# Chunked attention and a top-1 mixture of experts: row transposes placed between the halves of two matmul groups, and weight loads given to later groups

## The chip, the cores and the metric

The kernel runs on one core of a Trainium2 chip. The metric is the device time of one launch in microseconds (us); smaller is better. The engines named below are PE (matrix multiplies and transposes; PEld is its loading of weights), DVE (vector), ACT (scalar, activation), POOL (general purpose, it also issues the scattering and gathering DMAs) and SP (it only issues DMAs).

## The reference

Attention is computed in chunks of 64 positions, for 8 batches, 8 heads, 576 positions and a head size of 64. Its 4608 rows of 512 numbers go through a mixture of 8 experts, where each row uses only the expert with the largest gate logit.

```python
scores = scale * np.matmul(q_c, k_c.transpose(0, 1, 2, 4, 3))
attn = np.exp(scores - np.max(scores, axis=-1, keepdims=True))
attn = attn / (np.sum(attn, axis=-1, keepdims=True) + 1e-09)
x = np.matmul(attn, v_c)                    # -> rows: (4608, 512)
logits = x @ w_gate                         # (4608, 8)
expert_idx = np.argmax(logits, axis=1)
for e in range(8):
    xe = x[expert_idx == e]
    out[expert_idx == e] = gate_w * (np.maximum(xe @ w1[e], 0.0) @ w2[e])
```

Everything is float32. The experts' first layer is 512 to 1024 wide, the second 1024 to 512.

## The kernel before, in words

The rows are cut into 36 tiles of 128 and taken in 18 groups `g` of two tiles. One pass of the loop `for g in range(NG)` (line 1069) is a software pipeline in which four groups are under way. The names of its stages, with their lines:

- `scores(g)` (L255): 64 small matmuls of q and k into the two PSUM banks `psS`. The softmax follows on DVE and ACT: `soft_a` takes the maxima `mx` (L268) and subtracts them (`ex`, L271), `soft_b` is the exponential on ACT (L277), `soft_c` the sums `su` (L281), `soft_d` their reciprocals `ri` (L292).
- `attn_t` (L300) transposes the exponentials of group g-1 on PE, one PSUM bank for each tile, and ACT copies each bank to `at`.
- `attn_v` (L309) multiplies them by v into the banks `psU` and `psV`; `x_out` on DVE (L321, one instruction for each bank) scales them by `ri` and writes the rows `xb`.
- `x_t` (L332) transposes the rows of group g-2, one bank for each tile, and ACT copies them to `xT`; `logits` (L344) multiplies by the gate weights, and ACT copies the result `lp` (L1041).
- `sel_` (L1032) of group g-3 turns the logits into the layout of the routing, whose small steps (`advance`, `small_op`) lie on DVE; `store` (L451, POOL) scatters the rows to their experts' places `xd`, and after the 18 stores of the first batches gathers read them again (L583, POOL).

The transposes of `attn_t` use the banks U and V in the loop, those of `x_t` the banks T and Q. Every group reads 512 KB each of q (L208), k (L211) and v (L229) through SP's queue.

Beside this, the loop brings in the first expert's weights. `load_c(j)` (L1054) is one 512 KB DMA into half of a `raw` tile. The loads 0 to 3 are the first layer. `split_half` cuts each into two halves and each half into a rounded part `whi` (ACT, L88) and the rest `wlo` (POOL, L90), eight halves in all; the POOL part stands a group behind the ACT part. The loads 4 to 7 are the second layer and take the place of the raw first layer, so each has to wait until the `wlo` of its half is done. `loads` and `splits` say in which group each is called. From 124 us on PE also computes the first blocks of experts (L662) between the last groups, and from 161 us it computes nothing else.

On PE, DVE, ACT and POOL the instructions stand in the order of the code. On SP a scheduler decides the order: a load stands there as early as its waits let it, and not where the code calls it.

Of the kernel before, what the change touches and what calls it, by code (L numbers as in the profile page):

```python
# [8 lines left out]
F32 = mybir.dt.float32  # L9
# [9 lines left out]
P = 128  # L19
# [5 lines left out]
G = 2  # L25
NG = NTILE // G
RB = 4
XB = 5
# [21 lines left out]
def attn_moe_kernel(ctx: ExitStack, tc: tile.TileContext, q, k, v, wg, w, out):  # L50
# [192 lines left out]
            nc.tensor.matmul(pR.rearrange("p (a b) -> p a b", b=P), ones,  # L243
                             ones.unsqueeze(1).broadcast_to([P, 4, P]), start=True, stop=True)

    def scores(g):
        ps = pair
        if g == 3:
            nc.tensor.addr_align(64, offset=48, max_nops=0)
        for i in range(G):  # L250
            if g == 0 and i:
                keep(3)
            for hp in range(4):
                for po, m, fo, pi, fi, at_ in quads(i, hp):
                    nc.tensor.matmul(ps[po, m, fo], qt[g][pi, i, fi], kb[g % NK][pi, i, fi],  # L255
                                     start=True, stop=True, tile_position=at_)
        return ps
# [34 lines left out]
        nc.vector.reciprocal(ri.rearrange("p h o -> p (h o)"), suf)  # L292
        return ri

    def attn_t(ex, banks="UV"):
        at = sp.tile([P, G, 4, 128], F32, name="at", bufs=1)
        for i in range(G):
            pt = bank(banks, [P, 4, 128])
            for hp in range(4):
                nc.tensor.transpose(pt[:, hp, :], ex[:, i * 4 + hp, :, :].rearrange("p m k -> p (m k)"), ident)  # L300
            nc.scalar.copy(at[:, i, :, :], pt)
        return at

    def attn_v(g, at):
        px = [one["U"], one["V"]]
        for i in range(G):
            for hp in range(4):
                for po, m, fo, pi, fi, at_ in quads(i, hp):
                    nc.tensor.matmul(px[m][po, fo], at[pi, i, hp, po], vb[g % NB][pi, i, fi],  # L309
                                     start=True, stop=True, tile_position=at_)  # L310
        return px
# [12 lines left out]
                ri[:, m * NH // 2:(m + 1) * NH // 2, :].rearrange("p (i h) o -> p i h o", i=G)  # L324
                .broadcast_to([P, G, 4, 64]), ALU.mult)

    def x_t(g, xt):
        xT = sp.tile([P, 4, G * P], F32, name="xT1", bufs=1)
        for i in range(G):
            pxt = bank("TQ", [P, 4, 128])  # L330
            for kc in range(4):
                nc.tensor.transpose(pxt[:, kc, :], xt[:, (g * G + i) % RB, kc * 128:(kc + 1) * 128],  # L332
                                    ident)
            nc.scalar.copy(xT[:, :, i * P:(i + 1) * P], pxt)
        return xT
# [124 lines left out]
    def advance(kind, side=False):  # L460


        for x in active:
            if x[1] == kind and x[2] == side and not (kind == "t" and r_live[0]):
                x[1] = next(x[0], "end")
                if x[1] == "end":
                    active.remove(x)
                return
# [582 lines left out]
    def load_c(j):  # L1051

        c, s = j // 2, slice(j % 2 * F, (j % 2 + 1) * F)
        nc.sync.dma_start(raw[c % 2][:, s], w[c * E * P:c * E * P + P, s])  # L1054

    loads = {0: [1], 2: [2], 4: [3], 15: [4], 16: [5], 17: [6, 7]}
    splits = {g: [g - 1] for g in range(1, 9)}

    def cast(g):

# [3 lines left out]
        for j in loads.get(g, ()):  # L1064
            load_c(j)

    load_c(0)

    for g in range(NG):
        ga, gl = g - 1, g - 2  # L1070
        pace[0] = 1000
        if waiting:
            nc.gpsimd.tensor_copy(relay, st_l[gl - 1][:, 0:1])
        store(1 if g + 2 < NG else 4)
        ps = scores(g)
        keep((8, 6, 0)[min(g, 2)])

        if gl >= 1:
            sel_(gl - 1)
            advance("c")  # L1080
        if ga >= 0:
            at = attn_t(st_e[ga])
            if g + 3 < NG:
                hold_q(g + 3)
            su = soft_c(st_e.pop(ga))
        if gl >= 0:
            st_x[gl] = x_t(gl, xb[gl * G // RB % XB])
        if ga >= 0:
            soft_e(su)
        st_e[g] = soft_a(ps)  # L1090
        if g + 1 < NG:
            soft_b(st_e[g])
        else:

            c2.close()
            psum = ctx.enter_context(tc.tile_pool(name="psum", bufs=1, space=PSUM))
            slots["S"] = [psum.tile([P, 512], F32, name=f"psS{i}") for i in range(2)]
            turns["S"] = 0
        pauses()
        for x in casts:  # L1100
            next(x, None)
        casts.clear()
        advance("t")
        if g + 1 < NG:
            small_op(5)
        if ga >= 0:
            px = attn_v(ga, at)
        logits(gl)
        cast(g)
        if g + 1 == NG:  # L1110
            soft_b(st_e[g])
        if ga >= 0:
            ri = soft_d(su)
            x_out(ga, px, ri, xb[ga * G // RB % XB])
        small_op(2)
        advance("a")
        side_op(4)
        if waiting and g + 2 < NG:
            nc.gpsimd.tensor_copy(relay, st_e[g][:, 0, 0, 0:1])
            store(1)  # L1120
        if g + 3 < NG:
            load_q(g + 3)
        if 3 <= g + 2 < NG:
            load_v(g + 2)
        if g + 3 < NG:
            if gl >= 0:
                hold(kb[(g + 3) % NK])
            load_k(g + 3)
# [4 lines left out]
    make_xt(0, banks="SS")  # L1133
    small_op(5)
    ex = st_e.pop(g)
    at = attn_t(ex, "TQ")
    filler(1)
    su = soft_c(ex)
    soft_e(su)
# [220 lines left out]
```

## Time and profile before

| | |
|---|---|
| median of the runs | 579.99 us |
| profiled execution, its time | 575.24 us |
| its span (first to last instruction) | 573.1 us, granted PE clock 0.994 of full speed |
| PE, PEld busy | 95%, 83% of the span |
| DVE, ACT, POOL busy | 73%, 49%, 41% |
| chain that ended last, by engine | PE 83%, issue 7%, DVE 5%, DMA 2% |

The profiled execution lies 4.75 us under the median. "Issue" in a chain of waits is time in which an engine waited for nothing that the profile shows. A window is a stretch of the span, given by its first and last microsecond. In a row of a timeline, the brackets hold the idle time before the instruction and what ended it.

### The profile page before, as it was taken

To read this page: it belongs to the slowest core of one execution; us is meant where nothing else is said; L and a number is where in the kernel's file an instruction comes from. 1 tells how busy PE (TensorE), PEld (TensorE's weight loads), DVE (VectorE), ACT (ScalarE), POOL (GpSimd) and SP (SyncE) were. 2 spreads that over 40 slices of the span, in tenths; PEclk is the share of its full clock that TensorE was granted. 3 is DMA by queue.
4 is the path that set the end of the run, shared out by engine and by line. 5 is a ranking of instruction groups with operands and counts; after the bars stand their busy time and mean duration, and the time that the engine had idled before them with its cause. 6 is when DMAs were issued, how large, how long until landed. Compare 5 with 4: busy or idle time off the path is not lost.

```text
span 573.1 us, 14350 instructions
## 1 busy us (share of the span) xinstructions
PE 544.2 (95%) x5315; PEld 475.3 (83%) x5315; DVE 421.1 (73%) x886; ACT 278.2 (49%) x502; POOL 232.2 (41%) x272
## 2 busy tenths in 40 slices
PE   7698688899999999999999999999999999999995
PEld 4586667687689889898898999898999989899984
DVE  6789797995688887798877885667656566756654
ACT  1486555564163654456545553445425344544432
POOL 3114533366455445263542643152424226151422
PEclk9999998999999999999999999999999999999998
DMA  8989997843358452335625632466622346211201
GB/s 309 399 311 335 340 357 253 332 154 153 123 178 302 156 195 64 83 115 175 202 72 203 219 114 88 145 225 210 219 65 84 120 130 224 74 45 24 73 2 57
DMA packets 44852, 99.28 MB, mean 173 GB/s; under 512 B 12736, under 2 KB 26048, under 8 KB 41152
## 3 DMA queue, kind: packets, MB, share of 16 engines
q0 software_dynamic: 18352, 58.30, 29.3%
q1 hardware_dynamic: 26384, 39.36, 20.5%
q8 instruction: 83, 1.36, 1.0%
q14 instruction: 33, 0.27, 0.1%
HBM read 106.59 MB, written 20.22 MB: 221 GB/s over the span
## 4 chain that ended last, share of the span: by engine, by line
PE 83%; issue 7%; DVE 5%; DMA 2%; ACT 1%; POOL 1%; SPq 0%; POOLq 0%; DVEq 0%; ACTq 0%
PE psS L662 27%; PE psL L662 8%; PE psV L746 4%; PE psU L746 4%; PE psU L748 4%; PE psU L747 4%; PE psV L747 4%; PE psV L748 4%; PE psS L255 2%; PE psU L309 2%; PE psK L760 2%; PE psK L762 2%; DMA qt<-in_q 1%; PE psK L747 1%; PE psK L748 1%
## 5 line engine op out<-in xcount | busy, mean ns | idle before, releaser
L80 DVE TENSOR_TENSOR wlo<-raw,whi 128x1024 fp32r<-128x1024 f32 x114 | 138.8, 1218 | 14.6 <-ACT whi L79 14.1
L557 POOL DMA_INDIRECT raw<-in_w,widx x58 | 68.3, 1177 | 126.1 <-DVE wlo L80 57.8
L79 ACT CAST whi<-raw 128x1024 fp32r<-128x1024 f32 x114 | 118.8, 1043 | 0.0
L695 ACT ACTIVATE h<-psS 128x384 fp32r<-128x384 f32 x84 | 41.3, 492 | 158.8 <-issue 120.3
L662 PE MATMUL psS<-xhi,whi 128*128 128x256 f32 (+3 forms) x368 | 114.8, 314 | 0.1
L662 PE MATMUL psS<-xhi,wlo 128*128 128x256 f32 (+3 forms) x368 | 112.2, 307 | 0.0
L662 PE MATMUL psS<-xlo,whi 128*128 128x256 f32 (+3 forms) x368 | 106.3, 307 | 0.2 <-DVE xlo L613 0.2
L779 POOL DMA_INDIRECT out_y<-y,oid x40 | 43.0, 1076 | 100.3 <-ACTq L1247 34.6
L666 DVE SCALAR_TENSOR_TENSOR hl<-psS,h 128x256 fp32r<-128x256 f32 x84 | 35.5, 422 | 57.9 <-ACT h L695 57.8
L662 PEld LDWEIGHTS psS<-xhi,whi 128*128 128x128 f32 x368 | 69.4, 189 | 5.7 <-issue 1.6
L662 PEld LDWEIGHTS psS<-xhi,wlo 128*128 128x128 f32 x368 | 69.5, 189 | 4.0 <-issue 1.2
L575 POOL DMA_INDIRECT xg<-xd,idx x47 | 59.8, 1273 | 23.8 <-issue 12.2
L662 PEld LDWEIGHTS psS<-xlo,whi 128*128 128x128 f32 x368 | 67.6, 189 | 0.5 <-DVE xlo L613 0.4
L746 PE MATMUL psU<-whi,h 128*128 128x512 f32 x112 | 45.1, 403 | 0.0
L746 PE MATMUL psV<-whi,h 128*128 128x512 f32 x112 | 44.3, 396 | 0.0
L748 PE MATMUL psU<-whi,hl 128*128 128x512 f32 x112 | 44.0, 392 | 0.0
L747 PE MATMUL psU<-wlo,h 128*128 128x512 f32 x112 | 43.9, 392 | 0.0
L747 PE MATMUL psV<-wlo,h 128*128 128x512 f32 x112 | 43.8, 391 | 0.0
L748 PE MATMUL psV<-whi,hl 128*128 128x512 f32 x112 | 43.8, 391 | 0.0
L451 POOL DMA_INDIRECT xd<-xb,di x32 | 31.5, 986 | 14.0 <-issue 4.3
L662 PE MATMUL psL<-xhi,whi 128*128 128x384 f32 (+3 forms) x112 | 34.7, 310 | 0.2 <-issue 0.2
L255 PEld LDWEIGHTS psS<-kb,qt 64*64 64x64 f32 x1152 | 20.0, 137 | 17.8 <-issue 10.6
(259 smaller groups left out, 1133.8 us busy)
## 6 DMA issues: line engine op xcount, KB each, us to landing
vb<-in_v SPq DMA_DIRECT2D x18, 512.0 KB
kb<-in_k SPq DMA_DIRECT2D x17, 512.0 KB
qt<-in_q SPq DMA_DIRECT2D x17, 512.0 KB
xg<-xg SPq DMA_DIRECT2D x208, 32.0 KB
raw<-in_w SPq DMA_DIRECT2D x8, 512.0 KB
raw<-in_w,widx POOLq DMA_INDIRECT x58, 3.2
xg<-xd,idx POOLq DMA_INDIRECT x49, 3.9
out_y<-y,oid POOLq DMA_INDIRECT x40, 3.1
```

What stands on the lines that cost most here:

```text
L79: nc.scalar.copy(hi, src)
L80: nc.vector.tensor_tensor(lo, src, hi.bitcast(F32), ALU.subtract)
L451: landed[t] = nc.gpsimd.indirect_dma_start(out=xds[t], out_offset=bass.IndirectOffsetOnAxis(ap=di[:, i, :], axis=0), in_=x, in_offset=None ...
L557: nc.gpsimd.indirect_dma_start(out=raw[c][:, :], out_offset=None, in_=w, in_offset=bass.IndirectOffsetOnAxis(ap=widx[:, u, c:c + 1], axis= ...
L575: nc.gpsimd.indirect_dma_start(out=t[:, :], out_offset=None, in_=xd[0:rows, :], in_offset=bass.IndirectOffsetOnAxis(ap=place(u, h), axis=0 ...
L662: nc.tensor.matmul(ph, a[par][kc][:, f * 128:(f + 1) * 128], b[:, kc, at_:at_ + ph.shape[1]], start=kc == 0 and n == 0, stop=kc == 3 and n ...
L666: nc.vector.scalar_tensor_tensor(o, ph, 0.0, hi.bitcast(F32), ALU.max, ALU.subtract)
L695: nc.scalar.activation(hx[:, EXT:EXT + WIDE], ph, AF.Relu)
L746: nc.tensor.matmul(py, hh, wh, start=f == 0, stop=False)
L747: nc.tensor.matmul(py, hh, wl, start=False, stop=False)
L748: nc.tensor.matmul(py, hl, wh, start=False, stop=f == 7)
L779: nc.gpsimd.indirect_dma_start(out=outs[m], out_offset=bass.IndirectOffsetOnAxis(ap=oid[u % 3][:, m:m + 1], axis=0), in_=y, in_offset=None ...
```

## The change

It has two parts. First, the order on PE within a group. The half of `x_t` that belongs to the first tile stands between the two tiles' halves of `scores`, the other half between the two halves of `attn_v`; `sel_` stands behind `attn_t` instead of ahead of it; and `attn_t` uses the banks T and Q, as `x_t` does. Second, the groups in which the first expert's weights are called: the first layer's four loads in groups 11 to 14 and its splits in groups 13 to 16, two halves each, instead of one half in each of the groups 1 to 8. The second layer's calls stay in groups 15 to 17.

```diff
-    def scores(g):
+    def scores(g, part=range(G)):
...
-        for i in range(G):
+        for i in part:
...
-    def attn_t(ex, banks="UV"):
+    def attn_t(ex, banks="TQ"):
...
-    def attn_v(g, at):
+    def attn_v(g, at, part=range(G)):
...
-    def x_t(g, xt):
-        xT = sp.tile([P, 4, G * P], F32, name="xT1", bufs=1)
-        for i in range(G):
+    def x_t(g, xt, part=range(G), xT=None):
+        if xT is None:
+            xT = sp.tile([P, 4, G * P], F32, name="xT1", bufs=1)
+        for i in part:
...
-    loads = {0: [1], 2: [2], 4: [3], 15: [4], 16: [5], 17: [6, 7]}
-    splits = {g: [g - 1] for g in range(1, 9)}
+    loads = {11: [0], 12: [1], 13: [2], 14: [3], 15: [4], 16: [5], 17: [6, 7]}
+    splits = {13 + i: [2 * i, 2 * i + 1] for i in range(4)}
...
-    load_c(0)
...
-        ps = scores(g)
+        ps = scores(g, [0])
+        if gl >= 0:
+            xt_l = xb[gl * G // RB % XB]
+            st_x[gl] = x_t(gl, xt_l, [0])
+        scores(g, [1])
         keep((8, 6, 0)[min(g, 2)])
-
-        if gl >= 1:
-            sel_(gl - 1)
-            advance("c")
         if ga >= 0:
             at = attn_t(st_e[ga])
             if g + 3 < NG:
                 hold_q(g + 3)
             su = soft_c(st_e.pop(ga))
-        if gl >= 0:
-            st_x[gl] = x_t(gl, xb[gl * G // RB % XB])
+        if gl >= 1:
+            sel_(gl - 1)
+            advance("c")
         if ga >= 0:
             soft_e(su)
+            px = attn_v(ga, at, [0])
+        if gl >= 0:
+            x_t(gl, xt_l, [1], st_x[gl])
...
         if ga >= 0:
-            px = attn_v(ga, at)
+            attn_v(ga, at, [1])
         logits(gl)
```

On PE, one group reads so before (group 3, at whose start `L249` sets an address). The 32 rows L309 of `attn_v` that follow are left out.

```order
 L249 ISA
-L255 MATMUL psS<-kb_127,qt 64x64 x32
-L1032 MATMUL psL<-sel_g,lp 128x8 x2
-L300 MATMUL psU<-ident,ex 128x128 x4
-L300 MATMUL psV<-ident,ex 128x128 x4
-L332 MATMUL psT<-ident,xb_123 128x128 x4
-L332 MATMUL psQ<-ident,xb_123 128x128 x4
+L255 MATMUL psS<-kb_127,qt 64x64 x16
+L333 MATMUL psT<-ident,xb_123 128x128 x4
+L255 MATMUL psS<-kb_127,qt 64x64 x16
+L300 MATMUL psQ<-ident,ex 128x128 x4
+L300 MATMUL psT<-ident,ex 128x128 x4
+L1033 MATMUL psL<-sel_g,lp 128x8 x2
```

The instructions are the same in number. The first four transposes of rows have moved from behind `attn_t` to the middle of `scores`; the other four (not shown) stand behind the first sixteen rows L309.

On SP the first layer's loads do not stand at the end of the loop. Their place is early in the program, behind the k of group 4 (the first row) and ahead of the q of group 7 (`raw_66` and `raw_67` are the two raw tiles).

```order
L211 DMA kb_128<-in_k 128x1024
L1055 DMA raw_66<-in_w 128x1024
L208 DMA qt<-in_q 128x1024
L229 DMA vb_131<-in_v 128x1024
L211 DMA kb_129<-in_k 128x1024
L1055 DMA raw_66<-in_w 128x1024
L208 DMA qt<-in_q 128x1024
L1055 DMA raw_67<-in_w 128x1024
L229 DMA vb_132<-in_v 128x1024
L211 DMA kb_127<-in_k 128x1024
L1055 DMA raw_67<-in_w 128x1024
```

Before, two of these four stood further ahead, in front of the q of group 3, and the other two behind the k of group 4 and the k of group 6. The second layer's loads, which stood between the q, k and v of the middle groups, now stand at the very end of SP's rows:

```order
L1055 DMA raw_66<-in_w 128x1024
L208 DMA qt<-in_q 128x1024
L229 DMA vb_131<-in_v 128x1024
L211 DMA kb_129<-in_k 128x1024
L1055 DMA raw_66<-in_w 128x1024
L229 DMA vb_132<-in_v 128x1024
L1055 DMA raw_67<-in_w 128x1024 x2
```

The q in the second row is that of the last group, and each of the four loads waits for a `wlo` of POOL.

On POOL the eight L90 instructions stood one by one between the stores of groups 2 to 9. After the change they stand in pairs between the last stores and gathers:

```order
L366 COPY ft<-pid 128x6
L90 TENSOR_TENSOR wlo_0_76<-raw_66,whi_0_68 128x512 x2
L1123 COPY relay<-ex 128x1
L452 DMA xd<-xg_64,di 4608x528
L1073 COPY relay<-lp 128x1
L452 DMA xd<-xg_64,di 4608x528
L584 DMA xg_64<-xd,idx_229 128x528 x2
L90 TENSOR_TENSOR wlo_1_77<-raw_66,whi_1_69 128x512 x2
```

The first pair has come between a routing copy and the stores of group 14, the second behind the two gathers. The third pair follows in the same way behind the next routing copy, and the fourth behind one more store, ahead of the copy L366 that ends the loop's stores.

## Rows read from the trace of the kernel before

**Rows 1.** Windows: stretch, busy us (count) of PE, PEld, DVE, ACT, POOL, PEclk, DMA, GB/s
```profile
11.95:55.66 43.71, 37.26 (x1083) 30.58 (x1083) 36.48 (x53) 27.24 (x68) 10.72 (x14) 1.00 0.95 355
55.66:93.89 38.23, 29.03 (x803) 25.01 (x799) 29.53 (x55) 20.34 (x54) 15.65 (x31) 0.96 0.90 322
93.89:124.10 30.21, 27.37 (x800) 23.22 (x796) 28.65 (x60) 18.32 (x49) 15.71 (x28) 1.00 0.78 274
161.40:573.00 411.60, 405.26 (x2269) 365.16 (x2268) 297.23 (x592) 197.23 (x291) 168.64 (x143) 1.00 0.41 135
87.50:94.00 6.50, 6.49 (x123) 5.85 (x125) 4.11 (x9) 3.49 (x7) 0.87 (x5) 0.74 0.66 234
```

**Rows 2.** Chain in order of time, 51 to 86 us: start us, us, what
```profile
51.71 1.11 issue
...
63.50 2.00 issue
...
71.73 0.57 PE psL L344 x8
72.30 1.09 PE psS L255 x64
73.39 0.54 PE psL L1032 x4
...
74.86 0.44 PE psT L332 x4
...
85.28 2.23 issue
```

**Rows 3.** Window between the ends of two stalls of PE, columns as in rows 1
```profile
58.53:65.48 6.95, 4.96 (x127) 4.14 (x127) 5.96 (x13) 4.36 (x12) 3.43 (x6) 1.00 0.99 364
```

**Rows 4.** DMA traffic from 58.54 to 63.2 us
```profile
DMA packets 434, 1.60 MB, mean 343 GB/s; under 512 B 47, under 2 KB 47, under 8 KB 433
```

**Rows 5.** DMA queue of instructions from 63.2 to 63.3 us: packets, MB, share
```profile
q8 instruction: 1, 0.02, 54.9%
```

**Rows 6.** Timeline of SP's DMA issues: start us, us, line, tiles
```profile
9.05 1.62 SPq L1054 DMA_DIRECT2D raw<-in_w  x2
...
38.83 1.06 SPq L1054 DMA_DIRECT2D raw<-in_w  x1
...
44.29 0.38 SPq L1054 DMA_DIRECT2D raw<-in_w  x1
...
54.70 0.33 SPq L1054 DMA_DIRECT2D raw<-in_w  x1
...
67.93 0.33 SPq L1054 DMA_DIRECT2D raw<-in_w  x1
...
102.48 0.33 SPq L208 DMA_DIRECT2D qt<-in_q  x1
```

**Rows 7.** Timeline of DVE in one group: start us, us, line, tiles
```profile
71.77 0.69 DVE L321 TENSOR_TENSOR xg<-psU,ri 128x512 f32<-128x512 f32 x1 [1.71 <-PE psV L309]
72.37 0.68 DVE L321 TENSOR_TENSOR xg<-psV,ri 128x512 f32<-128x512 f32 x1
...
74.10 1.21 DVE L268 TENSOR_REDUCE mx<-psS 128x16 f32<-128x1024 f32 x1
...
77.11 0.69 DVE L321 TENSOR_TENSOR xg<-psU,ri 128x512 f32<-128x512 f32 x1
```

**Rows 8.** Timeline of POOL from group 14 on
```profile
105.61 0.18 POOL L1119 COPY relay<-ex 128x1 f32<-128x1 f32 x1 [2.52 <-ACT ex L277]
...
113.80 1.05 POOL L583 DMA_INDIRECT xg<-xd,idx  x1 [5.14 <-issue]
...
124.61 0.20 POOL L365 COPY ft<-pid 128x4 f32<-128x4 f32 x1
```

**Rows 9.** POOL instructions grouped by line: count, busy us, mean ns, idle before
```profile
L90 POOL TENSOR_TENSOR wlo<-raw,whi 128x512 fp32r<-128x512 f32 x8 | 10.2, 1277 | 33.1 <-ACT whi L88 27.7 <-ACT kb L214 5.4
```

**Rows 10.** Timeline of PE, the fourth block of first-layer weights
```profile
130.63 0.28 PE L662 MATMUL psS<-xhi,wlo 128*128 128x256 f32 x1
```

More of the change, by code (lines that the diff above doesn't have):

```diff
@@ L244, in keep @@
                              ones.unsqueeze(1).broadcast_to([P, 4, P]), start=True, stop=True)
-    def scores(g):
+    def scores(g, part=range(G)):
         ps = pair
-        if g == 3:
+        if g == 3 and part[0] == 0:
             nc.tensor.addr_align(64, offset=48, max_nops=0)
-        for i in range(G):
+        for i in part:
             if g == 0 and i:
@@ L325, in x_out @@
                 .broadcast_to([P, G, 4, 64]), ALU.mult)
-    def x_t(g, xt):
-        xT = sp.tile([P, 4, G * P], F32, name="xT1", bufs=1)
-        for i in range(G):
+    def x_t(g, xt, part=range(G), xT=None):
+        if xT is None:
+            xT = sp.tile([P, 4, G * P], F32, name="xT1", bufs=1)
+        for i in part:
             pxt = bank("TQ", [P, 4, 128])
@@ L1135, in attn_moe_kernel @@
     ex = st_e.pop(g)
-    at = attn_t(ex, "TQ")
+    at = attn_t(ex)
     filler(1)
```

## The prediction, made before the changed kernel was run

> **What bounds the kernel now.** I first read the busy time by windows [rows 1]. From 161.40 us to the end PE works 405.26 of 411.60 us. The change leaves that stretch as it is, so it can only move it as a block. What can be won or lost lies in the loop, in three stretches. From 11.95 to 93.89 us (81.94 us) no engine is full: PE has 37.26 + 29.03 = 66.29 us of work and DVE 36.48 + 29.53 = 66.01, while the DMA engines are 95% and 90% busy. From 93.89 to 124.10 us DVE sets the pace with 28.65 of 30.21 us (95%).
>
> Then the chain of waits [rows 2] says what PE waits for in the first two stretches: "issue", so nothing that the profile ties to another engine. The standstills lie about a group apart and last 1 to 2 us. Between the ends of two of them PE has executed 127 matmuls [rows 3] (128 with the record that is missing), so the stops come after a fixed number of instructions: PE waits for its next block of instructions. In the stretch between 58.54 us, where PE goes on, and 63.2 us no packet of the instruction queue for that block moves, while the data queues move 1.60 MB [rows 4]; then its packet comes [rows 5], and PE goes on at 65.50 us. So the block waits behind data already queued, and the length of a standstill depends on how many bytes were queued when PE asked. Clearing the queue ahead of this one took 1.60 MB / 0.343 MB per us = 4.7 us; one 512 KB load in it is 0.524 / 0.343 = 1.5 us of that.
>
> A rule of the Trainium skill speaks against this reading. Its page "Runtime: NRT & Kernel Launch", section "Instruction fetch mechanics", says that PE's instructions come in blocks of 256 (128 matmuls with their weight loads, which fits the trace), but that crossing a block is "mostly hidden". The trace disagrees, with 2.00 us at one crossing [rows 2]; by the rule the first term below would be zero.
>
> **The change, part by part,** against the profiled execution's 575.24 us; the median of the runs, 579.99, lies 4.75 above it.
>
> *Loads that leave the middle of the loop.* The second layer's four loads, at 38.83, 44.29, 54.70 and 67.93 us [rows 6], leave the middle for the last groups. Two of them lie ahead of a block that PE had to wait for: that of the standstill at 51.71 (1.11 us) was asked for shortly after the load of 44.29, that of 63.50 (2.00 us), asked for where PE went on at 58.54, after the load of 54.70 [rows 2, 6]. A standstill can shrink by no more than itself and by no more than a load's 1.5 us: 1.11 + 1.5 = **-2.6 us**. Bounds: 0, if other data take the gap at once, and 4 x 1.5 = -6.0.
>
> *First-layer loads.* The code calls them in groups 11 to 14, but SP's order puts them behind the k of group 4 to ahead of the q of group 7. So two leave 9.05 us [rows 6] and two more come to about 19 to 34 us, where blocks wait behind them in the same way. One for one this is **0**, with one load's 1.5 us to either side.
>
> *The slow clock.* From 87.5 to 94.0 us the granted clock is 0.74 while PE is busy throughout, so 0.26 x 6.50 = 1.7 us are lost there [rows 1]; ahead of it PE stood for 2.23 us, the longest of the standstills [rows 2]. The change moves the standstills about and may take this drop away or make another: **0**, +-1.7.
>
> *Row transposes earlier.* The rows of `x_t` come from `x_out`. Before, they were ready with time to spare: `x_out` ended at 72.37 + 0.68 = 73.05 us [rows 7], and the transposes began at 74.86 [rows 2], 1.8 us later. Now the first half comes after the logits and half of the scores. `attn_v` ends at 71.73, plus 0.57 and half of 1.09 us [rows 2], is 72.85. `x_out` begins 0.04 us after `attn_v`, so the semaphore back to PE arrives about 73.09: PE waits 0.24 us in each of 16 groups, 3.8 us at most. Behind that wait stand the rest of the scores, for which DVE's `mx` waits: 73.09 + 0.44 + 0.55 = 74.08 us, and `mx` began at 74.10 [rows 7]. So DVE, whose group takes 77.11 - 71.77 = 5.34 us, is just not held up by this. Where PE stands before its next block anyway, the wait is inside that standstill, since the block comes when its data come. I take half, **+1.9 us** (0 to 3.8). `sel_` behind `attn_t` covers ACT's copies with its 0.54 us [rows 2], so the copies cost nothing there; without this cover an ACT instruction (18.32 / 49 = 0.37 us [rows 1]) would stand on the path.
>
> *Four loads in a bunch.* The first of the second layer's loads now waits for the first pair of `wlo` subtractions. They are 2 x 1.28 us [rows 9] and fit into the 2.52 us in which POOL was idle before 105.61 [rows 8]. So it goes at about 105.7 us, and behind it in SP's queue stands the last q, which went at 102.48 [rows 6]. This q lands 3 us later, behind a load of 1.5 us, and blocks of instructions wait behind the loads too. In this stretch DVE sets the pace and the DMA share is 78% [rows 1], which covers most: **+1.0**, one block's wait being about the size; 0 to 3.
>
> *POOL's tail.* The second pair of subtractions (2.55 us) stands behind the gathers, after the 5.14 us wait [rows 8], so it pushes all that follows. POOL had ended its loop at 124.61 us; it now has 2.55 + 2.55 us more ahead and 1.28 for the first of the fourth pair: 130.99 us. PE needs that block at 130.63 [rows 10]: **+0.4 us**; 0 if DVE's pace lets POOL catch up, 1.9 if the gathers' wait also grows by a load (1.5).
>
> *Hidden.* ACT's casts of the first layer (in groups 13 to 16) meet an engine with 18.32 of 30.21 us busy, POOL's eight subtractions add 10.2 us to 15.71 of 30.21 [rows 1, 9]; both fit. The early stretches lose these, but there neither engine was the bound. Without the cover the cost is that of the POOL tail above.
>
> Sum: -2.6 + 0 + 0 + 1.9 + 1.0 + 0.4 = **+0.7 us**, so 575.9 for a profiled execution and **580.7 us** for the median.
>
> **Rivals.**
>
> *Faster, the standstills go.* If the lighter queues let most blocks arrive in time, the first two stretches run as the third does: 66.01 us of DVE work at 95% is 69.6 us where 81.94 were taken, 12.3 us less. For it: four loads of eight leave. Against it: q, k, v and the stores, which stay, still fill the DMA engines by far the most, and loads are added early. Half of it, with the other terms hidden, is -6.2: **573.8 us**.
>
> *Slower, the rows' wait.* If PE's wait for `x_out` is not covered and the copy of the first half stands behind another ACT instruction (0.37 us [rows 1]), so that `attn_t`'s second half waits for the bank T, each of 16 groups costs 0.24 + 0.37 = 0.61 us, 9.8 instead of 1.9. This decides once DVE's `mx` starts later than the 74.08 worked out above, since DVE then has the wait in its own round. For it: 0.02 us are left there. Against it: most groups have a standstill that swallows it. 580.7 + 7.9 = **588.6 us**.
>
> *The relief is nothing.* If the blocks' waits depend not on the loads but on the stores and on q, k and v, the first term is zero: 580.7 + 2.6 = **583.3 us**. The rule of the Trainium skill named above ("Runtime: NRT & Kernel Launch", "Instruction fetch mechanics") would give the same time; the standstill of 2.00 us speaks against it.
>
> **How the numbers follow.** My forecast has 0.54 (its own range is 577.3 to 584.7: in the terms of the leaving loads, the rows, the bunch and POOL half of the way to both bounds, -1.7 - 1.0 - 0.5 - 0.2 and +1.3 + 1.0 + 1.0 + 0.7), the faster rival 0.22, the rows' wait 0.16, no relief 0.08. The predicted time is the forecast's. The range reaches from 574.0 (half of the faster rival lies below: 0.11) to 588.0 (over half of the rows' wait lies above: 0.09), so 0.20 is left out. The 2% about which a measurement tells this kernel from no change lies at 568.4 and 591.6. Below would need 11.6 of the 12.3 us, above the rows' wait with all upper bounds: 0.03 each, 0.94 within.
>
> **What would show it.** In the profile after, between 38 and 68 us there must be no L1055, and the issue standstills near 50 and 63 us must be shorter by 1 to 1.5 us each; if not, the first term is wrong. Of the transposes L333 for bank T, PE should wait for DVE's `x_out` by about 0.2 us in groups without a standstill; waits above 0.5 us in most groups would be the slower rival. DVE's round in the last groups should stay at 5.3 to 5.4 us. L1055 should come at about 106 us with the last q behind it, and the matmul with the fourth `wlo` should wait on POOL at about 131 us. The forecast is wrong if standstills shift from the middle to the early or last groups by more than they shrink there.

## The result and the profile after

| | before | changed |
|---|---|---|
| median of the runs side by side | 579.8 us | 586.24 us |
| ratio, 95% interval | | 1.0147 (1.0116 to 1.0177) |
| profiled execution, its span | 575.24, 573.1 us | 587.53, 585.7 us |

A ratio compares, of each kernel, the runs that lie within 1.5% of its fastest.

The change makes the kernel 6.4 us slower, 1.5%. That is 5.5 us more than the 580.7 forecast. It lies inside the range, on the side of the slower rival, but not by that rival's mechanism, so that it lies there is luck. A second measurement on another chip (below) gave 1.011 (1.0075 to 1.0144).

The windows of the changed kernel, in the same stretches as [rows 1] (columns as there):

```profile
11.95:55.66 43.71, 39.70 (x981) 30.55 (x971) 32.81 (x49) 22.11 (x55) 1.70 (x5) 0.88 0.88 301
55.66:93.89 38.23, 34.66 (x903) 27.53 (x899) 33.03 (x62) 22.77 (x62) 14.37 (x32) 1.00 0.93 328
93.89:124.10 30.21, 26.10 (x656) 20.31 (x655) 24.47 (x47) 19.23 (x45) 14.28 (x20) 0.94 0.73 234
```

In the second row PE is busier, 34.66 us instead of 29.03, for 12% more matmuls. The clock's slow stretches have moved: 0.88 in the first row, which had 1.00, and 1.00 in the second, which had 0.96. Two further rows show what the stretch between the last group's scores and the third block of first-layer matmuls takes. The first is of the kernel before, the second of the changed one, same columns:

```profile
117.94:130.05 12.11, 11.26 (x266) 9.92 (x262) 11.29 (x32) 7.62 (x20) 5.93 (x12) 1.00 0.37 141
```

```profile
122.68:142.18 19.50, 13.42 (x265) 11.30 (x261) 17.03 (x35) 9.23 (x23) 13.62 (x22) 0.91 0.62 204
```

The same number of matmuls takes 7.4 us longer here, and DVE is busy for 5.7 us more with about the same instructions (35 rows for 32). This stretch, which I call the tail, explains a loss of the measured size by itself in this execution. The two profiled executions lie 12.3 us apart, and 4.7 us of that lie ahead of the tail. They are not put down to the change: the last group's scores began at 117.94 us in the kernel before and at 122.68 us here, but at 121.3 to 126.8 us in the profiles of the five kernels below whose time is that of the kernel before (the order on PE alone, the shape changes, the second layer's bytes left out, the second layer late with either order). Two long idle times of PE stand in the tail, in PE's timeline of the changed kernel (start, length, instruction, in brackets the idle time before it and what ended it):

```profile
125.67 0.33 PE L333 MATMUL psT<-ident,xb 128*128 128x128 f32 x1 [2.29 <-DVE xb L321]
...
137.99 0.40 PE L663 MATMUL psS<-xlo,whi 128*128 128x256 f32 x1 [2.94 <-DVE xlo L614]
```

Both wait for DVE. DVE's timeline of the same stretch shows why it is late:

```profile
121.57 2.40 DVE L375 TENSOR_TENSOR lg<-lg,lm 128x32 f32<-128x32 f32 x1
...
124.92 0.69 DVE L321 TENSOR_TENSOR xb<-psU,ri 128x512 f32<-128x512 f32 x1
...
132.26 1.28 DVE L417 TENSOR_SCALAR gs<-gs 128x4 f32<-128x4 f32 x1
...
134.41 2.93 DVE L603 SCALAR_TENSOR_TENSOR oid<-msk,xg 128x1 int32<-128x1 f32 x1
137.26 0.68 DVE L614 TENSOR_TENSOR xlo<-psS,xhi 128x512 fp32r<-128x512 f32 x1
```

L375 works on 128x32 numbers, L417 on 128x4, L603 on one column. Elsewhere such instructions take 0.14 to 0.21 us. Here they take 2.40, 1.28 and 2.93 us, and `x_out` (L321) and `xlo` (L614) stand behind them. At the same time POOL runs:

```profile
121.40 2.51 POOL L90 TENSOR_TENSOR wlo<-raw,whi 128x512 fp32r<-128x512 f32 x2
...
130.99 2.51 POOL L90 TENSOR_TENSOR wlo<-raw,whi 128x512 fp32r<-128x512 f32 x2
...
134.82 2.49 POOL L90 TENSOR_TENSOR wlo<-raw,whi 128x512 fp32r<-128x512 f32 x2
```

Each of the three long DVE instructions ends within 0.1 us of the end of one of these pairs (123.97 and 123.91, 133.54 and 133.50, 137.34 and 137.31). So the subtractions seem to hold them up, which the experiments below test. L603 begins 0.4 us before its pair is shown to begin; starts on POOL are rough, and whether something else of POOL's holds it at first stays open. Other DVE instructions beside POOL's subtractions take their usual time: the reductions (L415, 0.17 us; `mx`, 1.23 us) and those that read a PSUM bank (`ex`, 1.23 us; `x_out`, 0.68 us). In the kernel before, one small DVE instruction between 10 and 124 us takes longer than 0.35 us, and it too ends (45.05 us) with a subtraction (44.98 us), a single one:

```profile
44.38 0.67 DVE L389 TENSOR_TENSOR lo<-am,iota_m 128x48 bf16<-128x48 f32 x1
```

```profile
43.71 1.27 POOL L90 TENSOR_TENSOR wlo<-raw,whi 128x512 fp32r<-128x512 f32 x1 [4.07 <-ACT whi L88]
```

The other seven single subtractions [rows 9] met none of the routing's small instructions with inputs in SBUF.

The sum of the tail: 2.29 + 2.94 us of waiting, and 0.09 x 19.50 = 1.8 us by the clock, which fell behind the second wait, make 7.0 of the 7.4 us.

One more thing shows in a group in which PE never stands still, one row of the changed kernel and one of the kernel before (columns as in [rows 1]):

```profile
79.79:85.53 5.74, 5.69 (x161) 4.58 (x157) 5.37 (x11) 3.82 (x11) 2.53 (x5) 1.00 1.01 372
```

```profile
72.23:77.33 5.10, 5.10 (x161) 4.38 (x157) 4.78 (x7) 3.39 (x11) 1.55 (x3) 1.00 0.97 338
```

PE works through the same number of matmuls, 161, at the full clock, and needs 0.64 us more. PE's weight loads in that group, changed kernel, show where:

```profile
80.42 0.42 PEld L333 LDWEIGHTS psT<-ident,xg 128*128 128x128 f32 x4
81.00 0.56 PEld L255 LDWEIGHTS psS<-kb,qt 64*64 64x64 f32 x32 [0.17 <-issue]
```

Between the 128x128 transposes and the 64x64 matmuls the weight load stands for 0.17 us. The change has four more of these borders in a group, 8 for 4.

### The profile page after: what moved, and what is told of

Same layout as the page of the kernel before. It is cut to its first block, busy times and chain, and to the rows that moved or that the text cites. A ratio compares the mean times of both kernels' runs of the same rounds, so it can differ in the third digit from the quotient of the medians.

```text
span 585.7 us, 14319 instructions
## 1 busy us (share of the span) xinstructions
PE 558.0 (95%) x5315; PEld 480.7 (82%) x5315; DVE 426.4 (73%) x886; ACT 280.1 (48%) x502; POOL 234.6 (40%) x272
## 4 chain that ended last, share of the span: by engine, by line
PE 71%; issue 4%; DVE 1%; POOL 1%; ACT 0%; POOLq 0%; ACTq 0%
PE psS L663 26%; PE psL L663 8%; PE psV L747 4%; PE psU L747 4%; PE psU L749 4%; PE psU L748 4%; PE psV L748 4%; PE psV L749 4%; PE psK L761 2%; PE psK L763 2%; PE psK L748 1%; PE psK L749 1%; PE psK L747 1%; PE psV L708 1%; PE psU L708 1%
## 5 line engine op out<-in xcount | busy, mean ns | idle before, releaser
L558 POOL DMA_INDIRECT raw<-in_w,widx x58 | 70.0, 1207 | 123.3 <-DVE wlo L80 57.5
L255 PEld LDWEIGHTS psS<-kb,qt 64*64 64x64 f32 x1152 | 22.0, 141 | 16.4 <-issue 12.2
```

The costliest lines, as they stand in the source:

```text
L558: nc.gpsimd.indirect_dma_start(out=raw[c][:, :], out_offset=None, in_=w, in_offset=bass.IndirectOffsetOnAxis(ap=widx[:, u, c:c + 1], axis= ...
```

## The experiments

Three theories stood at the start. A: the changes of the matmul shape on PE cost about 0.16 us each. B: POOL's late pairs of subtractions hold up DVE. C: the wait of the row transposes for `x_out`, as in the slower rival of the prediction. Ratios are to the kernel before, run beside each kernel on the same chip, with the 95% interval.

**The changed order on PE alone.** The changed kernel with the old loads:

```diff
-    loads = {11: [0], 12: [1], 13: [2], 14: [3], 15: [4], 16: [5], 17: [6, 7]}
-    splits = {13 + i: [2 * i, 2 * i + 1] for i in range(4)}
+    loads = {0: [1], 2: [2], 4: [3], 15: [4], 16: [5], 17: [6, 7]}
+    splits = {g: [g - 1] for g in range(1, 9)}
...
+    load_c(0)
```

> The changed order on PE, with the loads and splits of the kernel before. Theory A (changes of the matmul shape on PE): after the change a group without a standstill took 5.74 us where it took 5.10 before, with the same instructions; between the 64x64 matmuls and the 128x128 transposes PE changes its shape four times more in a group, so it would be 0.16 us each. A expects stall-free groups of 5.7 us here too, and a time of 1 to 5 us over the kernel before, the rest of the 10 us being swallowed by shorter standstills. Theory B (the late splits): the 6.4 us come from POOL's subtractions in pairs among the last groups, beside which single DVE instructions took 2.4 to 2.9 us instead of 0.2. B expects the time of the kernel before within 1 us and no DVE instruction of that kind. Theory C (the rows' wait of the prediction): PE waits for x_out before the transposes in most groups, a sum of over 4 us; time 4 to 8 us over the kernel before.

Ratio 1.0011 (0.9977 to 1.0046): no difference. A's mechanism is there, a group without a standstill takes 5.78 us:

```profile
77.16:82.94 5.78, 5.73 (x160) 4.55 (x156) 5.14 (x7) 3.61 (x11) 2.17 (x3) 1.00 0.81 246
```

But the price does not reach the time. The idle times of PE that ended in "issue" sum to 11.5 us from 10 to 125 us, against 16.9 in the kernel before (8.2 in the changed one): the longer groups seem to use up time in which PE would have stood before its next block. That is a reading of one execution of each; 10 us of added work and 5.4 us less standing still do not balance. C falls too: the rows wait 1.1 us in all up to 125 us (1.6 in the changed kernel), and it costs nothing that can be measured. No small DVE instruction is held.

**The changed loads and splits alone.** The kernel before with the two new tables, `load_c(0)` taken out:

```diff
-    loads = {0: [1], 2: [2], 4: [3], 15: [4], 16: [5], 17: [6, 7]}
-    splits = {g: [g - 1] for g in range(1, 9)}
+    loads = {11: [0], 12: [1], 13: [2], 14: [3], 15: [4], 16: [5], 17: [6, 7]}
+    splits = {13 + i: [2 * i, 2 * i + 1] for i in range(4)}
...
-    load_c(0)
```

> The changed loads and splits, with the order on PE of the kernel before. Theory A (shape changes on PE): stall-free groups take 5.1 us and the time is that of the kernel before or 1 to 4 us less, since loads have left the middle. Theory B (late splits hold up DVE): the stretch from the last group to the first blocks of experts is 4 to 6 us longer, and the time 2 to 6 us over the kernel before, with small DVE instructions of 1.3 to 2.9 us beside POOL's subtractions. Theory C (rows' wait): time as before.

Ratio 1.0119 (1.0076 to 1.0162): the whole loss. The tail takes 19.45 us, and the held instructions are there (the lines are one less than in the changed kernel):

```profile
122.07 3.31 DVE L374 TENSOR_TENSOR lg<-lg,lm 128x32 f32<-128x32 f32 x1
...
133.18 1.74 DVE L416 TENSOR_SCALAR gs<-gs 128x4 f32<-128x4 f32 x1
...
135.50 3.23 DVE L602 SCALAR_TENSOR_TENSOR oid<-msk,xg 128x1 int32<-128x1 f32 x1
```

The sum of the standstills from 10 to 125 us is 18.5 us, although the second layer's loads have left the middle.

**The splits one by one.** The changed kernel with

```diff
-    loads = {11: [0], 12: [1], 13: [2], 14: [3], 15: [4], 16: [5], 17: [6, 7]}
-    splits = {13 + i: [2 * i, 2 * i + 1] for i in range(4)}
+    loads = {7: [0], 9: [1], 11: [2], 13: [3], 15: [4], 16: [5], 17: [6, 7]}
+    splits = {9 + i: [i] for i in range(8)}
```

> The changed kernel, but with one half split in each of the groups 9 to 16 instead of two in each of 13 to 16; POOL then has its eight subtractions one by one. Theory B (pairs of subtractions hold up DVE for up to 2.5 us and make rows and the first expert block late, 2.29 and 2.94 us of waiting PE): DVE's longest small instruction is at most 1.3 us, and the time is 3 to 5 us under that of the changed kernel, so 1 to 4 us over the kernel before. Theory A (shape changes on PE): the time of the changed kernel within 2 us, 4 to 8 over the kernel before, with stall-free groups of 5.7 us.

Ratio 1.0047 (1.0014 to 1.0079). Over half of the loss is gone, and one instruction is held for over 0.4 us (L417, 1.10 us). These are B's numbers. But the splits also come earlier here, and with them two of the second layer's loads (82.94 and 95.36 us, instead of 107.26 and 123.93), so this run alone does not tell the pairs from the lateness.

**Shape changes without anything else.** The kernel before, `sel_` between the halves of `scores`:

```diff
...
-        ps = scores(g)
+        ps = scores(g, [0])
+        if gl >= 1:
+            sel_(gl - 1)
+        scores(g, [1])
         keep((8, 6, 0)[min(g, 2)])
-
         if gl >= 1:
-            sel_(gl - 1)
             advance("c")
```

> The kernel before with one edit: the four matmuls of sel_ (128x8 out of full 128x128 weights) stand between the two halves of scores instead of behind them. No wait is added, PE has the same instructions, and its matmul shape changes twice more in a group. Theory A (shape changes at 0.16 us each): groups without a standstill take 5.10 + 0.32 = 5.4 us, and the time is 0 to 3 us over the kernel before. Theory C or B: stall-free groups stay at 5.10 us and the time is that of before.

A group without a standstill:

```profile
58.20:63.55 5.35, 5.35 (x160) 4.55 (x156) 5.04 (x9) 3.99 (x11) 3.62 (x5) 1.00 0.90 288
```

That is 5.35 us for 5.10: two more borders cost 0.25 us, 0.12 each, a little under the 0.16 of the changed kernel. The ratio is 0.9978 (0.9946 to 1.0011). As with the order on PE, the price is real in the group and absent in the time.

**The second layer's bytes left out.**

```diff
-        c, s = j // 2, slice(j % 2 * F, (j % 2 + 1) * F)
+        c, s = j // 2, slice(j % 2 * F, j % 2 * F + (F if j < 4 else F // 16))
```

> The kernel before, with the second layer's four loads of 512 KB cut to one sixteenth each (the rest of those weights is left out, so the second layer of the first expert is computed from other numbers). This measures the first term of the prediction by itself: 1.97 MB of 2.1 MB leave the middle of the loop and come nowhere else. As the prediction had it (standstills shrink by the bytes that were ahead of the block): 2.6 us faster, up to 6.0. Rival (the gap is filled by other data at once, and the next block still comes as late): within 1 us of the kernel before, the sum of the standstills from 38 to 94 us as before.

Ratio 0.9968 (0.9929 to 1.0007), -1.9 us with an interval from -4.1 to +0.4. The sum of the standstills from 10 to 125 us is 16.2 us, nearly the 16.9 before. At the 343 GB/s of [rows 4] the bytes left out are 5.7 us of DMA time (an estimate), so the loop does not simply follow the bytes that it moves. The run favours the prediction's -2.6 in the time and the rival in the standstills; it does not decide between them.

**The subtractions on DVE.** The changed kernel with

```diff
-            casts.append(split_half(j, nc.gpsimd))
+            casts.append(split_half(j, nc.vector))
```

> The changed kernel with the eight subtractions on DVE instead of POOL, in the same groups. Theory B (the pair on POOL holds up DVE's instructions with two inputs from SBUF): no small DVE instruction over 0.3 us in the last groups, PE waits under 0.5 us for x_out and for xlo, and from the start of the last group's scores to the third first-layer block of experts 14 to 16 us instead of 19.5; time 2 to 5 us under the changed kernel although DVE has about 5 us more work. Rival D (POOL's own delay, stores and gathers that come late, makes the tail long): the same, so it can't be told from B by the time, but by the DVE rows. Rival E (late casts on ACT or late loads make it): tail and time as the changed kernel, 585 to 588 us.

Ratio 1.0044 (0.9993 to 1.0096), from five of the twelve runs; the median of the twelve is 585.02 us, 5.0 over the 580.06 of the kernel before beside it. No small DVE instruction is held, as B said. But the tail is 17.5 us, not 14 to 16, and PE waits for `x_out`, ahead of which DVE now has the subtractions (0.68 us each):

```profile
125.29 0.44 PE L333 MATMUL psT<-ident,xb 128*128 128x128 f32 x2 [1.66 <-DVE xb L321]
```

So the run puts one delay of DVE in the place of another, and it does not decide whether late casts and late loads (E) make the loss. The next run, which keeps them, and the later ones do.

**POOL as busy, but reading nothing.** The changed kernel with

```diff
-        eng.tensor_tensor(lo, src, hi.bitcast(F32), ALU.subtract)
+        for n in (512, 512, 160):
+            eng.memset(lo[:, 0:n].bitcast(F32), 0.0)
```

> The changed kernel with POOL's subtractions replaced by memsets of about the same length (1.3 us for each half), which read nothing (the low parts of the first expert's first layer are zero, so that correction is left out). POOL is as busy and its stores and gathers as late as in the changed kernel. Theory B (two engines that read SBUF hold each other up): the DVE instructions with two inputs stay at 0.2 to 0.3 us, the tail is 14 to 16 us instead of 19.5 and the time 2 to 5 us under the changed kernel. Rival D (POOL's delay): tail about 19 us and the time of the changed kernel.

Ratio 1.0046 (1.001 to 1.0082). POOL's rows and DVE's in the same stretch:

```profile
123.86 2.75 POOL L91 MEMSET wlo<- 128x512 f32 x6
133.67 2.76 POOL L91 MEMSET wlo<- 128x512 f32 x6
137.93 2.75 POOL L91 MEMSET wlo<- 128x512 f32 x6
```

```profile
124.20 0.19 DVE L376 TENSOR_TENSOR lg<-lg,lm 128x32 f32<-128x32 f32 x1
135.45 0.17 DVE L418 TENSOR_SCALAR gs<-gs 128x4 f32<-128x4 f32 x1
...
138.32 0.15 DVE L604 SCALAR_TENSOR_TENSOR oid<-msk,xg 128x1 int32<-128x1 f32 x1
```

POOL is busy a little longer than before (2.75 for 2.51 us), DVE's same instructions run in the middle of it, and none is held. The tail is 13.2 us. This separates B from D and E: POOL's lateness, the late casts and the late loads together cost 2.7 us (0.6 to 4.8), and the rest goes with the subtractions.

**The splits in the middle of the loop.** The kernel before with

```diff
-    loads = {0: [1], 2: [2], 4: [3], 15: [4], 16: [5], 17: [6, 7]}
-    splits = {g: [g - 1] for g in range(1, 9)}
+    loads = {0: [1], 4: [2], 8: [3], 15: [4], 16: [5], 17: [6, 7]}
+    splits = {5 + i: [i] for i in range(8)}
```

> The kernel before with one edit: the eight splits, one by one, in groups 5 to 12 instead of 1 to 8, and the first layer's last two loads called in groups 4 and 8. Each second-layer load then goes out some four groups later, where the DMA engines have more room (78% after 94 us). If standstills follow the bytes that are queued, the time is 1 to 4 us under the kernel before. If single subtractions hold up DVE where it sets the pace (from 94 us on), it is 0 to 2 us over it. If neither matters, within 1 us.

Ratio 1.0043 (1.0012 to 1.0074), 2.5 us slower. Later loads bring no gain here either. No DVE instruction is held for over 0.3 us in this profile and its tail is 12.5 us, so the small loss is not explained.

**The pairs alone.** The kernel before, all of its own splits kept, with extra subtractions on POOL:

```diff
...
         casts.clear()
+        for _ in range(2 if g >= 14 else 0):
+            nc.gpsimd.tensor_tensor(spare, w_hi[0][0][:, 0:512].bitcast(F32), w_hi[0][0][:, 512:1024].bitcast(F32), ALU.subtract)
```

> The kernel before, all its loads and splits left as they are, with extra work on POOL alone: four pairs of subtractions 128x512 of two SBUF tiles into a spare tile, at the places where the changed kernel has its pairs. Theory B (the pairs hold up DVE's small instructions): DVE instructions of 1.3 to 3.3 us stand in the last groups, PE waits 2 to 4 us for xlo and up to 2 us for x_out, the stretch from the last group's scores to the third first-layer block takes 17 to 20 us instead of 12.1, and the time is 4 to 7 us over the kernel before. Rival F (what costs is that loads, casts and the second layer come late, and the holds would be hidden otherwise): tail within 2 us of 12.1, time within 2 us.

Ratio 1.0035 (1.0002 to 1.0069), 2.0 us where B said 4 to 7. DVE's instructions were held for 0.54 to 1.32 us only, and each was let in at the end of one subtraction. Two that began during the first of a pair (L416, 0.54 us; L374, 0.29 us) were let in between the two; in the changed kernel L375 was not. The two of a pair write the same tile here, those of the changed kernel do not; they also write another type (f32, not fp32r) and read other tiles. So the run left open what makes a hold long.

**The second layer late, splits early.** The kernel before with a one-element write ahead of the loads 4 to 7, which are called in groups 13 to 16:

```diff
+        if j >= 4:
+            nc.scalar.copy(raw[c % 2][0:1, j % 2 * F:j % 2 * F + 1], ident[0:1, 0:1])
...
-    loads = {0: [1], 2: [2], 4: [3], 15: [4], 16: [5], 17: [6, 7]}
+    loads = {0: [1], 2: [2], 4: [3], 13: [4], 14: [5], 15: [6], 16: [7]}
```

> The kernel before, whose second-layer loads are made to go out late by a one-element write on ACT in groups 13 to 16; splits and the first layer stay as they are. It tells the late loads from the late splits. If loads in the middle lengthen the standstills, as the prediction had it, and their lateness is hidden: 1 to 3 us under the kernel before, as with the bytes left out. If the standstills refill: within 1 us. If the late loads are what costs (the last q behind a load, four loads beside the gathers): 3 to 6 us over.

Ratio 0.9986 (0.995 to 1.0022); the loads went out at 104.19 us and later, and the standstills sum to 19.7 us. Neither the relief of the middle nor the bunch at the end moves the time by more than 0.5%.

**The changed order on PE with that.** The same edit in the kernel with the changed order on PE alone:

```diff
-    loads = {0: [1], 2: [2], 4: [3], 15: [4], 16: [5], 17: [6, 7]}
+    loads = {0: [1], 2: [2], 4: [3], 13: [4], 14: [5], 15: [6], 16: [7]}
```

> The changed order on PE, splits early as in the kernel before, second-layer loads late by the same write on ACT: the change's two ideas without the pairs on POOL. Theory A with the standstills as a cushion: within 3 us of the kernel before, groups without a standstill 5.7 us, the sum of standstills 8 to 12 us instead of 16 to 18. If the change's own ideas are worth something once the pairs are gone, 2 to 4 us under the kernel before.

Ratio 0.9998 (0.9971 to 1.0025), standstills of 10.9 us. Both ideas of the change without the pairs on POOL: no loss, and no gain.

**Pairs that write different places, and a gap in the pair.** The first is the kernel with extra pairs, but on the low parts themselves (`spare` is zero); the second the changed loads and splits alone, with a memset behind each subtraction:

```diff
...
+        for m in range(2 if g >= 14 else 0):
+            lo = w_lo[0][g - 14][:, m * 512:(m + 1) * 512]
+            nc.gpsimd.tensor_tensor(lo, lo.bitcast(F32), spare, ALU.subtract)
```

```diff
...
         for x in casts:
             next(x, None)
+            nc.gpsimd.memset(spare, 0.0)
```

> As the kernel with extra pairs, but the two subtractions of a pair write different halves (of the low parts themselves, from which a tile of zeros is subtracted, so the values stay as they are), as in the changed kernel; there, an instruction of DVE was held for up to 2.9 us, past the end of the pair's first subtraction, while with one spare tile for both it was let in between them. Theory B2 (a pair to different places leaves DVE no gap, so a hold lasts for what is left of the pair): holds of 1.3 to 3 us, tail 15 to 20 us instead of 12.1, time 3 to 7 us over the kernel before. Rival G (the gap has nothing to do with it; where DVE's instruction falls decides, and with the early loads it falls late): holds under 1.4 us, tail 13 to 14.5, time about 2 us over.

> The kernel with the changed loads and splits alone, with a small memset (128x256, reads nothing) on POOL behind each subtraction, so that the two of a pair are apart. Theory B2: DVE gets in behind the first subtraction; holds at most 1.4 us, tail 14 to 16 us instead of 19.5, time 1 to 4 us over the kernel before instead of 6.9. Rival G: holds, tail and time as without the memsets or a little longer, 5 to 8 us over the kernel before.

On the chip of these two the kernel before took 598.1 us. The ratios were 0.995 (0.9906 to 0.9994) and 0.9992 (0.9951 to 1.0034), so nothing was lost there although DVE was held for up to 3.17 us and the tails are 18.3 and 18.7 us long. In the first of them the hold of 3.17 us fell on L416 and not on L602, the `xlo` came in time, and PE waited only 0.9 us for DVE. PE's timeline has four idle times ending in "issue" in each of these tails, 2.2 and 1.6 us in all, of which the kernel before has none in its profile. No profile of the kernel before was taken on this chip, so why nothing was lost there stays open. Both were run again, beside the changed kernel and its loads alone, on one chip like the first:

> The changed kernel once more, beside the other three of this call on one chip, since the last two kernels ran on a chip whose instruction blocks came slower (the kernel before took 598 us there). Every theory: 1.0 to 1.8% over the kernel before if this chip is like the first; if it is like the last one, the number says how much of the holds is covered there.

> The changed loads and splits alone once more, on the chip of the other three. Theory B: 0.8 to 1.6% over the kernel before. If the time is within 0.3% of it, the first measurement owed to its chip.

> The kernel before with extra pairs of subtractions that write different halves, on the chip of the other three. Theory B2 (the hold is the cost, whatever the loads do): DVE holds of 1.3 to 3.2 us and 0.5 to 1.2% over the kernel before. Rival F (holds cost only where loads and casts are late too): under 0.4% over it.

> The changed loads and splits alone with a memset between the two subtractions of a pair, on the chip of the other three. In the run before, DVE's instruction stayed held through the memset to the end of the second subtraction (2.63 us). If that is so in general, the time is that of the loads alone, 0.8 to 1.6% over the kernel before; if the gap lets DVE in at most places, 0.2 to 0.7%.

| | ratio | 95% interval |
|---|---|---|
| changed kernel | 1.011 | 1.0075 to 1.0144 |
| loads and splits alone | 1.011 | 1.0066 to 1.0154 |
| extra pairs alone, different places | 1.0128 | 1.0083 to 1.0173 |
| loads and splits, memset in the pair | 1.0103 | 1.0067 to 1.0138 |

The third row is the strongest evidence for the cause. Everything is as in the kernel before, loads, casts, order on PE, and only POOL's pairs are added: on this chip the loss is as large as the changed kernel's. DVE, POOL and PE in that kernel:

```profile
133.09 1.08 DVE L416 TENSOR_SCALAR gs<-gs 128x4 f32<-128x4 f32 x1
...
135.17 2.80 DVE L602 SCALAR_TENSOR_TENSOR oid<-msk,xg 128x1 int32<-128x1 f32 x1
```

```profile
131.60 2.53 POOL L1107 TENSOR_TENSOR wlo<-wlo,spare 128x512 fp32r<-128x512 f32 x2
135.45 2.49 POOL L1107 TENSOR_TENSOR wlo<-wlo,spare 128x512 fp32r<-128x512 f32 x2
```

```profile
138.63 0.39 PE L662 MATMUL psS<-xlo,whi 128*128 128x256 f32 x1 [2.82 <-DVE xlo L613]
```

The chain is the same as in the changed kernel: one column of DVE is held for 2.80 us, `xlo` comes behind it, and PE waits 2.82 us. The memset in the pair does not help: holds of 2.30 and 2.56 us went through it. Why the pairs with one target held DVE for less stays open. So does part of the loss: the tails in these four profiles are 16.2, 16.0, 16.0 and 15.1 us, 2.9 to 4.1 over the 12.1 of the kernel before, while the four medians lie 5.4 to 7.7 us over it. The wait for `xlo` (`oid` in the last) is in all four. Where the rest lies, one profile of each kernel does not show.

## Why the prediction came out wrong

**What bounds the loop: it fits, but is not proven.** That PE's standstills before its blocks of instructions take up slack in the loop fits the changed order on PE, whose longer groups cost nothing. But less data did not shorten the standstills, so what sets their length stays open.

**Loads that leave the middle, -2.6 us: not confirmed.** Without those bytes the time moved by -1.9 us (-4.1 to +0.4), with the loads moved to the end by -0.8 (-2.9 to +1.3), and the sum of the standstills did not fall with them (16.9, 16.2, 19.7 us; 18.5 with the changed loads and splits alone). The step took two standstills of one execution and subtracted the load from each. Other data, it seems, take the gap: the rival of no relief was nearer. The Trainium skill's rule that crossing a block is mostly hidden ("Runtime: NRT & Kernel Launch", "Instruction fetch mechanics") does not explain it: every profile here has standstills of over 1.7 us.

**First-layer loads, 0: not measured by itself.** They went out at 19.00 to 35.71 us, where SP's order had put them, as predicted.

**The slow clock, 0 +- 1.7: too narrow.** In the changed kernel PE runs at half its clock from 30.0 to 34.5 us:

```profile
30.00:34.50 4.50, 4.50 (x79) 3.31 (x79) 0.93 (x3) 2.32 (x5) 0.00 (x0) 0.50 0.71 215
```

That alone loses 2.2 us, behind a standstill of 2.04 us, and the tail loses 1.8 behind the wait of 2.94 us. The forecast's own range counted neither this term's 1.7 nor the first-layer loads' 1.5. Such stretches come and go: the mean clock from 10 to 125 us is 0.91 to 0.94 in most profiles of the experiments, with either order on PE, and 0.99 in that of the kernel before, which lay 4.75 us under its median. Reading one term off one execution was the weak point.

**Row transposes earlier, +1.9 us: the wait's sum was near by luck, and another price was missed.** The rows waited 1.6 us in all for `x_out` from 10 to 124 us, by 0.13 to 0.29 us at a time, but in five groups and not by 0.24 us in each of 16, and the order on PE alone cost nothing that can be measured. What the step left out are the four more borders between matmul shapes, 0.64 us in each of 16 groups, 10.2 us of PE time. It priced a matmul by its duration alone and a moved one at nothing. By luck this does not show in the time. The Trainium skill has the rule (page "TensorEngine Tiling (Array Packing)", section "Key Properties": changing the tiling mode drains the TensorE). The traces agree and give 0.12 to 0.16 us for a border.

**Four loads in a bunch, +1.0 us: nothing measured.** The first pair of subtractions is 2 x 1.28 = 2.56 us and does not quite fit into POOL's 2.52, but SP did about what was said, L1055 at 107.26 us and the last q at 107.69:

```profile
107.26 0.33 SPq L1055 DMA_DIRECT2D raw<-in_w  x1
107.69 0.48 SPq L208 DMA_DIRECT2D qt<-in_q  x1
```

But the last scores did not wait for that q, and with the loads late alone nothing is lost (0.9986).

**POOL's tail, +0.4 us: this step failed.** The prediction asked whether PE waits for the fourth pair, and costed POOL's subtractions as POOL's time only ("both fit", under *Hidden*). PE did not wait for POOL in the tail. It waited for DVE, 2.29 and 2.94 us, which the pairs had held. Measured with only the pairs added the term is +5 to +10 us (1.0128, 1.0083 to 1.0173), ten times or more the 0.4; on the slower chip the same kernel lost nothing. The Trainium skill states the mechanism in "SBUF — State Buffer", section "SBUF: two separate sides": DVE instructions with two inputs from SBUF and a POOL instruction that reads SBUF exclude each other, and the loser waits. The traces agree for L375 and L603, which have two such inputs and were held for 2.40 and 2.93 us, and with the memsets, beside which they take 0.19 and 0.15 us. Two points it does not tell, and there the measurement decides: L417 has one such input and was held too (1.28 us), and L375 waited not for one whole instruction, as the page has it, but through two. I had looked at POOL's idle time and not at what DVE does beside it.

**The slower rival** had the right sign and a size near it, but its mechanism, the rows' wait behind an ACT copy, is not what happened. **The faster rival** fell: standstills halved (16.9 to 8.2 us) in the changed kernel, but with PE's own groups longer; with the changed loads alone they stayed (18.5 us).

**The slower chip.** The expectation for the changed kernel's second measurement says that instruction blocks came slower on the chip with 598.1 us. The profiles do not bear this out as the reason: from 10 us to the last group's scores the standstills sum to 14.9 and 17.6 us there, and to 16.9 us in the kernel before and 19.1 in the kernel with extra pairs on other chips. Only in the tail are there 2.2 and 1.6 us more.

## What to carry to other kernels

A move of work to an idle engine has two prices, its time there and what it holds up beside it. Before moving two-input work on POOL, list the DVE instructions that run at that time and what waits behind them: here a 0.2 us instruction in front of a critical one became a 3 us one. And where an engine stands still for its instructions anyway, work added to it may not show in the time, and work saved on it may bring nothing; measure the term alone before counting either.

## What the runs showed of the hardware

- A POOL subtraction of 128x512 from two SBUF tiles held small DVE instructions for up to 3.3 us, to the end of a pair of them, even with a 0.3 us memset between the two (2.30 and 2.56 us). Pairs that wrote the same tile held DVE for at most 1.32 us. Memsets of the same length on POOL held nothing. Reductions and instructions that read PSUM were not held beside subtractions (0.17, 0.68 and 1.23 us).
- A border between 64x64 and 128x128 matmuls costs PE 0.12 to 0.16 us at the full clock.
- PE's standstills before its blocks of instructions seem to act as a cushion: 10 us more of PE work in the loop left the time as it was (1.0011, 0.9977 to 1.0046).
- One chip took 598.1 us for the kernel that took 580 to 581 us on the others, and there the added pairs cost nothing (0.995, 0.9906 to 0.9994).
